# Preparing the last stage's first rows between two weight conversions, and taking two low planes to VectorE

## The chip, the cores and the metric

The kernel runs on one NeuronCore of a Trainium2 chip. The metric is the device time of one execution in microseconds (us). TensorE is PE in the profile, VectorE DVE, ScalarE ACT, GpSimd POOL, and SyncE SP; SP computes nothing here and requests most of the DMAs.

## The reference

A causal attention (4 batches, 12 heads, 448 positions, head dimension 64) gives 1792 rows of 768 numbers. A mixture of experts sends each row to one of 8 experts, and a last dense layer follows. Cut to what matters:

```python
x = softmax(q k^T / 8, causal) v                 # 1792 x 768
for e in range(8):                               # rows of expert e
    out[mask] = gate_w * eom * (relu(x[mask] @ w1[e]) @ w2[e])
h = out @ w_in                                   # 768 x 2048, float64 weights
y = (h - tanh(h)) @ w_out                        # 2048 x 768, float64 weights
```

## The kernel before

Each float32 operand is held as two float16 planes, a high one and a low one (the remainder), and each product is three float16 products. Work on PE goes in tiles of 128 rows.

The kernel has three stages in time: attention, experts, dense layer. In the expert stage the rows of an expert are handled in slots of 128 rows. `slot` (L815 and after) computes one slot: 144 matmuls with the expert's first weights (`slot_mm1`, tiles `ph`), the rectifier on ACT (L169, tile `hh`) with its remainder on DVE (L170, tile `hl`), and 48 matmuls with the second weights (`slot_mm2`, tiles `py`), whose result ACT copies (L831) and SP stores into `ys_d`, a buffer in device memory (L858). Slots past an expert's first ones stand in nested conditionals (`extra`, L871); expert 7 runs two slots here, one static and one `extra`.

The dense layer's weights come as 24 units of 128 x 1024 float64 numbers. A unit is loaded (`conv_load`, L906), turned into float32 by bit operations on DVE (`to_f32`, L896, L899, L902, through the buffer `cc`), scaled into its high plane (L113 on ACT or L117 on DVE), and its low plane is formed by `rest_of`: one DVE instruction (L121), or two on POOL for each half (L115 into the scratch `scm`, then the subtraction L129). `conv_store` (L917) writes 22 of the units back to `wb_d` in device memory. `conv` is all of this for one unit. The last two units are loaded on POOL's DMA queue into `stg` (named `wo` in the trace), and stay on the chip.

The order around the change is the order in which the program writes the instructions; each engine runs its own in that order. In front of expert 7 stands a conditional loop for leftover units (`remaining`, L1077); its body does not run with these inputs, but each engine takes the jump around it. The three 128-row blocks that the dense layer begins with (group 0) are requested by `prep0` (L971). During expert 7's static slot, `fill(1)` converts one unit, `fill(2)` requests the last two units and converts the second, and `fill(3)` runs `first_prep`: per block a maximum (L982), five short instructions for a scale (L984 to L989), the high plane on ACT (L996), the low plane in two halves on POOL (L1010, L1012), and short scale work on DVE (L1016 to L1025). Behind the slot SP requests the first chunk of the dense layer's first weights (`wi_load`, L955, two planes into `raw`) from `wb_d`, and the rows of group 1.

After the `extra` slot the block at L1181 to L1189 converts the last two units on DVE. Then PE transposes group 0 (L149, copied by ACT L153 and DVE L151), and the dense layer starts: `a_mm(n)` (L1222) makes the 16 tiles of a group, and DVE, ACT and POOL compute the cubic-like activation of each tile (DVE L1230 first, POOL L1232 and L1235, DVE L1242, L1248, L1250). The second product (L1273) of a group runs beside the first product of the next.

Of the kernel before, what the change touches and what calls it, by code (L numbers as in the profile page):

```python
# [12 lines left out]
F32 = mybir.dt.float32  # L13
# [3 lines left out]
U32 = mybir.dt.uint32  # L17
AF = mybir.ActivationFunctionType
ALU = mybir.AluOpType
AX = mybir.AxisListType  # L20
PSUM = bass.MemoryType.PSUM
SP = mybir.EngineType.SP
# [7 lines left out]
NBLK = NT // 128  # L30
# [16 lines left out]
NDY = 22  # L47
# [10 lines left out]
def build(ctx: ExitStack, tc: tile.TileContext, kq0, kq, v, wg, wo, w1, w2, wf, out):  # L58
# [26 lines left out]
    cst0 = cst.tile([1, E], I32, name="cst0")  # L85
    xtab = cst.tile([1, UOFF[-1]], I32, name="xtab")
    flg = cst.tile([1, 4], I32, name="flg")

    xTs = {"n0": cst.tile([128, 2, KD, 128], F16, name="xT_n0")}

# [817 lines left out]
    def conv(src, hi, lo, eng="v"):  # L908
        hs = [slice(0, 512), slice(512, 1024)]
        to_f32([(cc[:, h], src[:, h, :]) for h in hs])  # L910
        for h in hs:
            scaled("a", hi[:, h], cc[:, h].bitcast(F32))
        for h in hs:
            rest_of(eng, lo[:, h], cc[:, h].bitcast(F32), hi[:, h])
# [149 lines left out]
    def order_b():  # L1064
        px = mp_t.tile([128, 512], F32, tag="t", name="order")[:, 0 : 5 * NBLK]
        for c in range(NC_):
            nc.tensor.matmul(out=px, lhsT=oba[:, c, :], rhs=obb[:, c].rearrange("p n z -> p (n z)"), start=(c == 0),
                             stop=(c == NC_ - 1))
        pv = px.rearrange("p (n z) -> p n z", z=5)
        nc.vector.tensor_reduce(out=smt[:, :, 0:1], in_=pv[:, :, 0:2], op=ALU.add, axis=AX.X)  # L1070
        nc.vector.tensor_reduce(out=smt[:, :, 1:2], in_=pv[:, :, 2:5], op=ALU.add, axis=AX.X)

    wts = {0: wts0, 1: wts1 + w_tiles(1, (1,))}
    tl = tail()

    def remaining():
        with tc.If(tot < NDY):  # L1077
            with tc.For_i(tot, NDY, 1) as o:
                conv_load(stg[0], o)
                conv(stg[0], stg[2][:, 0:1024], stg[2][:, 1024:2048])  # L1080
                nc.sync.dma_start(out=wb_d[:, :, ds(o, 1), :].rearrange("p a o n -> p a (o n)"),
                                  in_=stg[2][:, 0:2048].rearrange("p (a n) -> p a n", a=2))

    cntrs = []
    for e in range(E):
        if e == 0:
            slot_rows(0, 2, 1)
            slot_rows(1, 0, "n")
        slot_rows(e, 2 + FB[e], 0)
        if e == 0:  # L1090
            for _ in range(4):
                next(tl, None)
        if e + 1 < E:
            if e:
                wts[e + 1] = w_tiles(e + 1)

            def fill_hi(z, e=e):
                todo = PLANS[e]
                if e:
                    pieces_hi(wts[e + 1], sum(todo, [])[CUT[z] : CUT[z + 1]])  # L1100
                else:
                    pieces_hi(wts[e + 1], todo[max(z - 1, 0)] if z != 1 else [])

            def fill_lo(z, e=e):
                if e == 0 and z >= 2:
                    next(tl, None)
                pieces(wts[e + 1], PLANS[e][z], e + 2, False)
                if e == 1 and z in (1, 3):
                    order_a(2) if z == 1 else order_b()

            fill = (fill_hi, fill_lo)
        else:
            wo_ = [w16s[0][z].tile([128, KF2, DM], F16, tag=tg, name=f"wo_{z}") for z, tg in enumerate(("w1", "w2"))]
            wof = [t.rearrange("p k f -> p (k f)") for t in wo_]
            stg = [wof[0][:, z * 4096 : (z + 1) * 4096].bitcast(U32).rearrange("p (n t) -> p n t", t=2) for z in range(2)]
            stg += [wof[1][:, z * 2048 : (z + 1) * 2048] for z in range(2)]
            tot = nc.values_load(flg[0:1, 1:2], min_val=0, max_val=NDY)
            remaining()
            first["yg"] = [wof[1][:, z * 2 * DM : (z + 1) * 2 * DM].bitcast(F32) for z in range(3)]
            at_ = (wof[1][:, 6 * DM :], wof[0])  # L1120
            first["yq"] = [[t[:, z * 2 * DM : (z + 1) * 2 * DM].rearrange("p (k x n) -> p k x n", k=KD, x=2)
                            for z in range(3)] for t in at_]
            first["dg"] = [[t[:, 6 * DM + 256 * z : 6 * DM + 256 * (z + 1)].bitcast(BF16).rearrange(
                "p (a n) -> p a n", a=2) for z in range(3)] for t in at_]
            first["sc"] = [t[:, 6 * DM + 768 : 6 * DM + 832].bitcast(F32) for t in at_]
            second = nc.values_load(flg[0:1, 0:1], engines=(SP,), min_val=0, max_val=128)
            for i in range(GB[0]):
                prep0(0, i, second * i if i else 0)

            def fill(z):  # L1130
                if z == 2:
                    for q in range(2):
                        conv_load(stg[q], NDY + q, nc.gpsimd)
                if z in (1, 2):
                    conv(cu[z - 1], co[z - 1][:, 0], co[z - 1][:, 1], "p")
                    conv_store(z - 1, nc.values_load(flg[0:1, z + 1 : z + 2], engines=(SP,), min_val=0, max_val=NDY - 1))
                if z == 3:
                    first_prep()

        if e == 0:  # L1140
            cntrs += [nc.values_load(cnt[0:1, x : x + 1], min_val=0, max_val=NT) for x in range(E)]
        cntr = cntrs[e]
        hint(e, 1 + FB[e])
        slot(e, FB[e], wts[e], f"n{e % 2}", fill,
             ((1, (FB[e] + 1) % 2),) + ((("n", f"n{(e + 1) % 2}"),) if e + 1 < E else ()),
             [lambda j=j: slot_rows(*j) for j in ((e + 1, 1, 1), (e + 2, 0, "n")) if j[0] < E], late=e + 1 == E)
        if e == 0:
            for _ in tl:
                pass
            sctx.close()  # L1150
            cv = w16ctx.enter_context(tc.tile_pool(reuse_waits="tile", name="cv", bufs=1, side="right"))
            cu = [cv.tile([128, 1024, 2], U32, name=f"cu_{z}") for z in range(2)]
            cc = cv.tile([128, 1024], U32, name="cc")
            co = [cv.tile([128, 2, 1024], F16, name=f"co_{z}") for z in range(2)]
            cuf = [t.rearrange("p n t -> p (n t)").bitcast(F16) for t in cu]
            cof = [t.rearrange("p a n -> p (a n)") for t in co]
            ccf = cc.bitcast(F32)
            ny = KD * 384
            spare = [t[:, ny:4096].bitcast(F32) for t in cuf]
            yg1 = cof[1][:, 0 : 2 * DM].bitcast(F32)  # L1160
            dgs = [cof[1][:, 1536 + 256 * z : 1792 + 256 * z].bitcast(BF16).rearrange("p (a n) -> p a n", a=2) for z in range(2)]
            rss = [cof[0][:, 768 * z : 768 * (z + 1)].bitcast(BF16).rearrange("p (a n) -> p a n", a=2) for z in range(2)]
            sc = [cof[0][:, 1536 + 64 * z : 1600 + 64 * z].bitcast(F32) for z in range(2)]
            G = {0: {"yh": cuf[0][:, 0:ny].rearrange("p (k n) -> p k n", k=KD),
                     "yl": cuf[1][:, 0:ny].rearrange("p (k n) -> p k n", k=KD), "rs": rss[0]}}
            oba = cof[1][:CP, 0 : NC_ * 128].bitcast(BF16).rearrange("p (c n) -> p c n", n=128)
            ob = ccf[:CP, 0 : 3 * NC_ * NBLK].bitcast(BF16)
            obm = ob[:, 0 : NC_ * NBLK].rearrange("p (c n) -> p c n", c=NC_)
            obb = ob[:, NC_ * NBLK :].rearrange("p (c n z) -> p c n z", c=NC_, z=5)
            order_a(0)  # L1170
            order_a(1)
            conv_load(cu[0], 0)
            conv_load(cu[1], unit_of(1, 1))
        if e == E - 1:
            wi_load(nc.sync, 0)
            for i in range(GB[1]):
                prep0(1, i, second * (GB[0] + i))
        extra(e, 1 + FB[e], wts[e])
    qc = (cc, wof[0][:, 8192:10240].bitcast(U32))
    qhl = [[y[:, (10 + q) * 1024 : (11 + q) * 1024] for y in wof] for q in range(2)]  # L1180
    for q in range(2):  # L1181
        to_f32([(qc[q], stg[q])])
        scaled("v", qhl[q][0], qc[q].bitcast(F32))
        if q:
            for prep in (prep2, prep3):
                for i in range(GB[0]):
                    tpool[0] = (mp_t, mp_y, mp_h)[i]
                    prep(0, i, "tys"[i])
        rest_of("p", qhl[q][1], qc[q].bitcast(F32), qhl[q][0])  # L1189

    mctx.close()
    gt = [w16s[1][z].tile([128, 2, KF2, 384], F16, tag=tg, name=f"g_{z}") for z, tg in enumerate(("w1", "w2"))]
# [10 lines left out]
    fp_o = wctx.enter_context(tc.tile_pool(reuse_waits="tile", name="fp_o", bufs=2, space=PSUM))  # L1203
    tpool[0] = wctx.enter_context(tc.tile_pool(reuse_waits="tile", name="fp_t", bufs=2, space=PSUM))

    oidx = yp.tile([128, NBLK, 2], U32, name="oidx")
    for z in range(2):
        nc.gpsimd.tensor_scalar(out=oidx[:, :, z], in0=smt[:, :, 0], scalar1=2.0, scalar2=float(z), op0=ALU.mult, op1=ALU.add)
    Q = {}
    ro = fp_o.tile([128, 512], F32, tag="o", name="ro")  # L1210
    for i in range(GB[0]):
# [171 lines left out]
```

## Time and profile before

| | |
|---|---|
| median of 3 runs | 1044.98 us (1041.18 to 1048.73) |
| profiled execution | 1040.45 us, span 1038.7 us |
| PE busy | 984.5 us, 95% of the span |
| DVE busy | 786.6 us, 76% |
| ACT busy | 596.7 us, 57% |
| POOL busy | 472.2 us, 45% |
| mean granted clock of TensorE | 0.993 |

The profile shows one execution. A row of the timeline gives the start from the beginning of the span, the length, the engine, the line, what is written and read, and in square brackets how long the engine had been idle and what released it. Rows of windows give what each engine was busy for in a stretch, then the granted clock of TensorE, then the share of the DMA engines' time and their rate.

### The profile page before, as it was taken

The numbers are of one execution on the slowest core, as the hardware profiler recorded it, in microseconds if no ns is written. First come the engines' busy times: TensorE is split into PE (matmuls) and PEld (weight loads), VectorE is DVE, ScalarE is ACT, GpSimd is POOL, SyncE is SP. The second block draws the span as 40 slices with busy tenths as digits, with TensorE's granted clock in tenths as the row PEclk, the third lists the DMA queues.
The fourth block names the chain that finished last, engine by engine and source line by source line (L and its number), as shares of the span: only waits on it lengthen the run. The fifth ranks groups of instructions, "written<-read, shape, count | busy, mean of one in ns | idle before, by whom it ended". The sixth has DMA issues, their size and how long they took to land. (4 is left out here: it accounts for less than half of the span.)

```text
span 1038.7 us, 24100 instructions
## 1 busy us (share of the span) xinstructions
PE 984.5 (95%) x9177; PEld 743.4 (72%) x9177; DVE 786.6 (76%) x1609; ACT 596.7 (57%) x1194; POOL 472.2 (45%) x499
## 2 busy tenths in 40 slices
PE   5999999998998999999988889999999999999996
PEld 4999999996876878777865555666666666667763
DVE  6668778786786778778877899887888798776640
ACT  5777776764456366564332679555656566555530
POOL 5475876585311011102137789545544443443321
PEclk9999999999999999999999999999999999999999
DMA  8989997963888979977987514010011000000000
GB/s 240 234 216 270 241 266 202 240 197 126 303 342 316 351 268 333 363 291 239 317 299 280 209 62 157 24 47 16 24 31 32 9 31 9 16 16 17 16 24 23
DMA packets 62646, 173.92 MB, mean 167 GB/s; under 512 B 8368, under 2 KB 23344, under 8 KB 59424
## 3 DMA queue, kind: packets, MB, share of 16 engines
q1 hardware_dynamic: 56352, 147.20, 42.7%
q0 software_dynamic: 6144, 24.84, 8.3%
q8 instruction: 79, 1.29, 0.5%
q14 instruction: 71, 0.58, 0.2%
HBM read 132.30 MB, written 29.62 MB: 156 GB/s over the span
## 5 line engine op out<-in xcount | busy, mean ns | idle before, releaser
L1273 PE MATMUL fo<-wo,g 128*128 128x384 f16 x1344 | 228.2, 326 | 0.0
L1222 PEld LDWEIGHTS <-raw 128*128 128x128 f16 x1440 | 140.7, 98 | 87.9 <-issue 9.5
L1273 PEld LDWEIGHTS <-g 128*128 128x128 f16 x1344 | 131.2, 98 | 83.8
L1232 POOL TENSOR_TENSOR V<-cu,cc 128x384 f32<-128x384 f32 (+1 forms) x80 | 78.7, 984 | 189.0 <-ACT cu L1231 188.2
L162 PEld LDWEIGHTS <-w 128*128 128x128 f16 x2592 | 148.9, 99 | 15.5 <-issue 14.4
L1222 PE MATMUL fh<-cu,raw 128*128 128x384 f16 (+1 forms) x864 | 131.9, 308 | 5.7 <-DVE cc L1230 5.7
L344 ACT ACTIVATE P<-s,nb 112x112 f32<-112x112 f32 (+1 forms) x192 | 89.9, 495 | 56.5 <-DVE nb L338 27.9
L381 PE MATMUL o<-v,PT 112*112 112x65 f32 x960 | 114.6, 259 | 0.0
L381 PEld LDWEIGHTS o<-v,PT 112*112 112x112 f32 x960 | 105.4, 178 | 0.1
L121 DVE SCALAR_TENSOR_TENSOR w<-raw,w 128x768 f16<-128x768 f32 (+1 forms) x99 | 99.1, 1061 | 3.6 <-ACT w L113 3.6
L799 POOL DMA_INDIRECT xg<-xs_d,idx x22 | 27.5, 1249 | 162.2 <-PEq L871 21.6
L1231 ACT ACTIVATE cu<-cc 128x384 f32<-128x384 f32 (+1 forms) x80 | 40.1, 502 | 101.9 <-DVE cc L1230 101.9
L1235 POOL TENSOR_TENSOR X<-cc,X 128x384 f32<-128x384 f32 (+1 forms) x80 | 91.2, 1141 | 4.1 <-ACT X L1234 0.5
L1230 DVE TENSOR_TENSOR cc<-fh,co 128x384 f32<-128x384 f32 (+1 forms) x80 | 42.0, 526 | 66.3 <-PE fh L1222 50.7
L113 ACT ACTIVATE w<-raw 128x768 f16<-128x768 f32 (+2 forms) x106 | 89.0, 904 | 5.5 <-DVE xi L758 3.2
L331 DVE TENSOR_REDUCE s<-s 112x2 f32<-112x224 f32 (+1 forms) x144 | 78.9, 548 | 14.8 <-PE s L327 12.7
L1242 DVE SCALAR_TENSOR_TENSOR V<-cu,V 128x384 f32<-128x384 f32 (+1 forms) x80 | 85.3, 1066 | 0.1
L1250 DVE TENSOR_TENSOR V<-V,co 128x384 f32<-128x384 f32 (+1 forms) x64 | 78.4, 1224 | 0.0
L1222 PE MATMUL fh<-yh,raw 128*128 128x384 f16 x384 | 67.6, 326 | 0.7 <-DVE cc L1230 0.7
L1251 ACT ACTIVATE g<-V 128x384 f16<-128x384 f32 (+1 forms) x80 | 40.1, 501 | 46.9 <-DVE V L1250 46.7
L362 PE MATMUL t<-ident,P 112*112 112x112 f32 x480 | 66.7, 262 | 0.0
L325 PE MATMUL s<-kh,qa 128*112 128x112 f16 (+1 forms) x192 | 54.7, 293 | 12.7 <-POOL qa L276 7.4
(657 smaller groups left out, 2038.8 us busy)
## 6 DMA issues: line engine op xcount, KB each, us to landing
raw<-w SPq DMA_DIRECT2D x48, 512.0 KB
raw<-w SPq DMA_DIRECT2D x60, 384.0 KB
cu<-wf SPq DMA_DIRECT2D x22, 1024.0 KB
wb_d<-co SPq DMA_DIRECT2D x22, 512.0 KB
raw<-kq SPq DMA_DIRECT2D x11, 896.0 KB
raw<-wb_d SPq DMA_DIRECT2D x8, 768.0 KB
xs_d<-xq SPq DMA_DIRECT2D x24, 224.0 KB
raw<-v SPq DMA_DIRECT2D x11, 448.0 KB
```

Source lines behind the costliest of these rows:

```text
L113: nc.scalar.activation(out=out, in_=in_, func=AF.Copy, scale=WS)
L121: nc.vector.scalar_tensor_tensor(out=out, in0=in_, scalar=WS, in1=hi, op0=ALU.mult, op1=ALU.subtract)
L162: nc.tensor.matmul(out=ph[:, (f % 4) * 128 : (f % 4 + 1) * 128], lhsT=w[0][:, ww, k, f * 128 : (f + 1) * 128], rhs=xTs[tag][:, xx, k, :], ...
L331: nc.vector.tensor_reduce(out=d["nm", m], in_=d["s", m], op=ALU.max, axis=AX.X, negate=True)
L344: nc.scalar.activation(out=d["P"][:, j, OFF[i] : OFF[i] + n], in_=d["s", m][:, z, :], func=AF.Exp, bias=d["nb"][:, 2 * i + j : 2 * i + j + ...
L381: nc.tensor.matmul(out=po[:, i, :], lhsT=d["PT"][:, g, o : o + CP], rhs=d["t"][3][:, hl, j, :], start=(j == 0), stop=(j == i))
L1222: nc.tensor.matmul(out=ph[:, 0:nt], lhsT=wi[ww][:, f // 4, k, f % 4 * 128 : (f % 4 + 1) * 128], rhs=yy[:, k, 0:nt], start=(q == 0), stop=( ...
L1232: nc.gpsimd.tensor_tensor(out=d["V"], in0=d["U"], in1=d["h"], op=ALU.mult)
L1235: nc.gpsimd.tensor_tensor(out=d["X"], in0=d["h"], in1=d["X"], op=ALU.subtract)
L1242: nc.vector.scalar_tensor_tensor(out=d["V"], in0=d[f"S{z}"], scalar=QD[z - 1], in1=d["V"], op0=ALU.add, op1=ALU.mult)
L1250: nc.vector.tensor_tensor(out=d["V"], in0=d["V"], in1=rs_y(g, nt), op=ALU.mult)
L1273: nc.tensor.matmul(out=po[:, 0:384], lhsT=t[:, x, k, i * 128 : (i + 1) * 128], rhs=wo_[ww][:, k, z * 384 : (z + 1) * 384], start=(k == 0 a ...
```

## The change

The three requests of group 0's rows come ahead of the conditional for leftover units; so that their buffer is not written by the loop, the loop's output goes to `spo`, another part of the weight buffer. `first_prep` moves from `fill(3)` to `fill(2)`, and the second conversion from `fill(2)` to `fill(3)`. The low planes of the last two units go from POOL to DVE, behind the transposes of group 0. The index table `oidx` for the output's scatter is made during expert 1.

```diff
+    oidx = cst.tile([128, NBLK, 2], U32, name="oidx")
...
+        for z in range(2):                       # now in order_b
+            nc.gpsimd.tensor_scalar(out=oidx[:, :, z], in0=smt[:, :, 0], scalar1=2.0, scalar2=float(z), op0=ALU.mult,
+                                    op1=ALU.add)
...
-                conv(stg[0], stg[2][:, 0:1024], stg[2][:, 1024:2048])
+                conv(stg[0], spo[:, 0:1024], spo[:, 1024:2048])
...
-            stg += [wof[1][:, z * 2048 : (z + 1) * 2048] for z in range(2)]
-            tot = nc.values_load(flg[0:1, 1:2], min_val=0, max_val=NDY)
-            remaining()
+            spo = wof[0][:, 8192:10240]
...
             for i in range(GB[0]):
                 prep0(0, i, second * i if i else 0)
+            tot = nc.values_load(flg[0:1, 1:2], min_val=0, max_val=NDY)
+            remaining()
 
             def fill(z):
                 if z == 2:
                     for q in range(2):
                         conv_load(stg[q], NDY + q, nc.gpsimd)
-                if z in (1, 2):
-                    conv(cu[z - 1], co[z - 1][:, 0], co[z - 1][:, 1], "p")
-                    conv_store(z - 1, nc.values_load(flg[0:1, z + 1 : z + 2], engines=(SP,), min_val=0, max_val=NDY - 1))
-                if z == 3:
                     first_prep()
+                if z in (1, 3):
+                    b = z // 2
+                    conv(cu[b], co[b][:, 0], co[b][:, 1], "p")
+                    conv_store(b, nc.values_load(flg[0:1, b + 2 : b + 3], engines=(SP,), min_val=0, max_val=NDY - 1))
...
         scaled("v", qhl[q][0], qc[q].bitcast(F32))
-        if q:
-            for prep in (prep2, prep3):
-                for i in range(GB[0]):
-                    tpool[0] = (mp_t, mp_y, mp_h)[i]
-                    prep(0, i, "tys"[i])
-        rest_of("p", qhl[q][1], qc[q].bitcast(F32), qhl[q][0])
+    for prep in (prep2, prep3):
+        for i in range(GB[0]):
+            tpool[0] = (mp_t, mp_y, mp_h)[i]
+            prep(0, i, "tys"[i])
+    for q in range(2):
+        rest_of("v", qhl[q][1], qc[q].bitcast(F32), qhl[q][0])
```

POOL's instructions in expert 7's static slot, before: the requests of the last two units (`wo<-wf`), the second unit's low plane (`co_4959`), then the blocks' low planes (`wo_17684`), of which the first half is shown.

```order
L906 DMA wo_17683<-wf 128x2048 x2
L115 TENSOR_SCALAR scm<-cc 128x512
L129 TENSOR_TENSOR co_4959<-scm,co_4959 128x512
L115 TENSOR_SCALAR scm<-cc 128x512
L129 TENSOR_TENSOR co_4959<-scm,co_4959 128x512
L1010 TENSOR_SCALAR scm<-wo_17684 128x384
L1012 TENSOR_TENSOR wo_17684<-scm,wo_17684 128x3x128
```

And POOL in the changed kernel, the end of the same place (the second unit is `co_4960` here, the blocks `wo_17687`):

```order
L1011 TENSOR_SCALAR scm<-wo_17687 128x384
L1013 TENSOR_TENSOR wo_17687<-scm,wo_17687 128x3x128
L116 TENSOR_SCALAR scm<-cc 128x512
L130 TENSOR_TENSOR co_4960<-scm,co_4960 128x512
L116 TENSOR_SCALAR scm<-cc 128x512
L130 TENSOR_TENSOR co_4960<-scm,co_4960 128x512
```

The second unit's low plane has moved behind all six halves of the blocks' low planes.

SP's instructions at the conditional, before: the end of the loop's body and the jump (L1078, L1077), then the three requests of rows.

```order
L1078 COMPARE_AND_BRANCH
L1078 UNCONDITIONAL_BRANCH
L1077 UNCONDITIONAL_BRANCH
L1126 TENSOR_LOAD flg
L1126 ISA x2
L971 DMA wo_17684<-ys_d 128x768
L971 ISA
L971 DMA wo_17684<-ys_d 128x768
L971 ISA
L971 DMA wo_17684<-ys_d 128x768
```

And SP in the changed kernel, up to the conditional's comparison (L1081):

```order
L1128 TENSOR_LOAD flg
L1128 ISA x2
L972 DMA wo_17687<-ys_d 128x768
L972 ISA
L972 DMA wo_17687<-ys_d 128x768
L972 ISA
L972 DMA wo_17687<-ys_d 128x768
L1131 TENSOR_LOAD flg
L1131 ISA x2
L1081 COMPARE_AND_BRANCH
```

The three requests have moved from behind the jump to a place ahead of its comparison; what follows on SP (two stores of units, the slot's store, `wi_load`, the rows of group 1) stands in the same order as before.

## Rows read from the trace of the kernel before

**Rows 1.** The page, the whole execution.

```profile
span 1038.7 us, 24100 instructions
```

**Rows 2.** Waits of PE: who waited for whom, us in total, times, longest.

```profile
PE py_I-18271_18272 L174 <- ACT hh_I-18095_18096 L169: 4.1, 1, 4.1
```

**Rows 3.** Timeline of PE: end of the extra slot, start of `a_mm`.

```profile
560.64 0.82 PE L174 MATMUL py_I-18271_18272<-w,hh_I-18095_18096 128*128 128x384 f16 x2 [4.07 <-ACT hh_I-18095_18096 L169]
...
574.50 8.94 PE L1222 MATMUL fh<-cu,raw 128*128 128x384 f16 x54
```

**Rows 4.** Windows: behind the wait, and late in group 0.

```profile
560.60:564.00 3.40, 3.35 (x11) 1.39 (x12) 2.89 (x5) 1.18 (x2) 3.10 (x4) 0.50 0.73 274
...
595.50:633.00 37.50, 33.95 (x220) 20.13 (x220) 37.50 (x59) 31.82 (x65) 33.18 (x31) 1.00 0.26 97
```

**Rows 5.** Timeline of ACT: high planes of group 0.

```profile
557.52 2.59 ACT L996 ACTIVATE wo<-wo 128x768 f16<-128x768 f32 x3 [5.63 <-issue]
```

**Rows 6.** Timeline of DVE: block preparation, last units, first tiles of group 0.

```profile
555.48 0.95 DVE L982 TENSOR_REDUCE wo<-wo 128x1 f32<-128x768 f32 x1 [2.96 <-DMA wo<-ys_d]
...
557.28 0.16 DVE L989 TENSOR_TENSOR wo<-wo,smt 128x3 f32<-128x3 f32 x1
...
565.08 1.82 DVE L902 SCALAR_TENSOR_TENSOR cc<-wo,cc 128x1024 uint32<-128x1024 uint32 x1
...
577.72 0.56 DVE L1230 TENSOR_TENSOR cc<-fh,co 128x384 f32<-128x384 f32 x1 [3.00 <-POOL scm L115]
...
581.30 0.92 DVE L987 TENSOR_SCALAR wo<-wo 128x3 f32<-128x3 f32 x1
...
582.47 0.70 DVE L989 TENSOR_TENSOR wo<-wo,smt 128x3 f32<-128x3 f32 x1
...
585.66 1.35 DVE L1242 SCALAR_TENSOR_TENSOR V<-S,V 128x384 f32<-128x384 f32 x1 [0.42 <-POOL V L1232]
```

**Rows 7.** Timeline of POOL: requests, low planes of the blocks and units.

```profile
548.38 1.18 POOL L906 DMA_DIRECT2D wo<-wf  x2
...
557.61 0.59 POOL L1010 TENSOR_SCALAR scm<-wo 128x384 f32<-128x384 f32 x1 [3.15 <-issue]
...
561.30 0.59 POOL L1010 TENSOR_SCALAR scm<-wo 128x384 f32<-128x384 f32 x1
561.97 0.91 POOL L1012 TENSOR_TENSOR wo<-scm,wo 128x384 f16<-128x384 f32 x1
562.98 1.00 POOL L1010 TENSOR_SCALAR scm<-wo 128x384 f32<-128x384 f32 x1
564.06 1.76 POOL L1012 TENSOR_TENSOR wo<-scm,wo 128x384 f16<-128x384 f32 x1
...
569.75 1.76 POOL L1012 TENSOR_TENSOR wo<-scm,wo 128x384 f16<-128x384 f32 x1
...
573.88 1.16 POOL L129 TENSOR_TENSOR wo<-scm,wo 128x512 f16<-128x512 f32 x1
575.13 0.62 POOL L115 TENSOR_SCALAR scm<-cc 128x512 f32<-128x512 f32 x1
```

**Rows 8.** Timeline of SP's queue: stores and loads as they are requested.

```profile
546.61 1.56 SPq L971 DMA_DIRECT2D wo<-ys_d  x3
...
559.95 0.56 SPq L917 DMA_DIRECT2D wb_d<-co  x1
...
563.43 0.83 SPq L955 DMA_DIRECT2D raw<-wb_d  x2
```

**Rows 9.** Line L1077 (the conditional) on SP: instruction, count, ns, first and last start.

```profile
L1077 SPq EVENT_SEMAPHORE  x2: 17/17/17, 545.6 to 545.7; - x2
...
L1077 SPq COMPARE_BRANCH  x1: 50/50/50, 541.6 to 541.6; - x1
```

**Rows 10.** Windows: a stretch of back-to-back loads; the last number is GB/s.

```profile
567.00:570.00 3.00, 3.00 (x21) 1.76 (x18) 2.97 (x3) 0.00 (x0) 2.73 (x4) 1.00 0.99 409
```

**Rows 11.** Groups by line: busy us, mean ns of one, idle before.

```profile
L121 DVE SCALAR_TENSOR_TENSOR w<-raw,w 128x1024 f16<-128x1024 f32 x41 | 48.1, 1216 | 0.0
```

More of the change, by code (lines that the diff above doesn't have):

```diff
@@ L1079, in remaining @@
                 conv_load(stg[0], o)
-                conv(stg[0], stg[2][:, 0:1024], stg[2][:, 1024:2048])
+                conv(stg[0], spo[:, 0:1024], spo[:, 1024:2048])
                 nc.sync.dma_start(out=wb_d[:, :, ds(o, 1), :].rearrange("p a o n -> p a (o n)"),
-                                  in_=stg[2][:, 0:2048].rearrange("p (a n) -> p a n", a=2))
+                                  in_=spo.rearrange("p (a n) -> p a n", a=2))
     cntrs = []
@@ L1204, in build @@
     tpool[0] = wctx.enter_context(tc.tile_pool(reuse_waits="tile", name="fp_t", bufs=2, space=PSUM))
-    oidx = yp.tile([128, NBLK, 2], U32, name="oidx")
-    for z in range(2):
-        nc.gpsimd.tensor_scalar(out=oidx[:, :, z], in0=smt[:, :, 0], scalar1=2.0, scalar2=float(z), op0=ALU.mult, op1=ALU.add)
     Q = {}
```

## The prediction

> **What bounds the kernel now.** I read the table of engines first: PE is busy for 95% of the span, so only a place where PE stands still, or where another engine sets the pace, can give or cost time. Then the waits of PE: one of 4.1 us stands at the place of this change [rows 2]. In PE's timeline it is the wait ahead of the extra slot's second product, 4.07 us to 560.64 [rows 3], and the window behind it shows a granted clock of 0.50 for 3.40 us, the lower of the two levels (1.2 instead of 2.4 GHz), so another 1.7 us of work lost [rows 4].
>
> Followed back: ACT's rectifier is queued behind three high planes of group 0, which begin at 557.52 [rows 5]; these wait for DVE's scale, ready at 557.44, behind a reduction that waited 2.96 us for the third block of rows [rows 6]. SP requests the rows from 546.61 on [rows 8], as it loses 4.0 us at the conditional, 541.6 to 545.6 [rows 9].
>
> What counts, though, is when DVE gets the first dense tile, at 577.72 [rows 6]: late in group 0 DVE is busy for 37.50 of 37.50 us [rows 4], so the group is DVE's from there, and a shift of that start goes 1:1 into the end. That start is a_mm(0) at 574.50 [rows 3] plus 3.22.
>
> **What the change does there.** *Rows earlier.* SP requests the blocks at about 541.7 instead of 546.61, 1.56 us for three. The third's reduction began 7.3 us after its request (555.48 - 548.17) beside POOL's loads, which are requested at 548.38 [rows 6 to 8]; a store of a unit is followed by its dependant after 3.48 (559.95 to 563.43 [rows 8]). From 543.3 the third block thus lands between 546.8 and 550.6; I take 547.1, since those loads still come behind the jump, now about 544.1 to 548.1. Adding 1.96 (555.48 to 557.44) the scale is ready at 549.0, and ACT is through with the high planes at 551.6 (2.59 [rows 5]). The second conversion now stands behind that on DVE; its three operations, 1.82 each at most [rows 6], end by about 557.3, the rectifier by about 558.5. PE's stall shrinks from 4.07 to about 2.2, and the drop of the clock there goes with it. PE is done with the slot some 3.5 us earlier.
>
> *The second unit later.* This is the price. On POOL the second unit's low plane now stands behind six halves of the blocks' low planes, and SP's store of that unit, requested at 559.95 before, waits for it. `wi_load` stands behind that store on SP and must see it land in `wb_d`. POOL is free for the halves at about 549.45 (jump, and the two loads of 1.18). A pair (scratch, subtraction) alone costs 0.59 + 0.91 + 2 x 0.08 = 1.66. Beside DVE's work on the last units three pairs took 562.98 to 571.51, 2.84 each [rows 7]. A half of the unit costs 0.62 + 1.16 + 0.16 = 1.94 alone, 3.3 at the same ratio. Bounds of POOL's end P: all alone 549.45 + 6 x 1.66 + 2 x 1.94 = 563.3; all contended 549.45 + 6 x 2.84 + 2 x 3.3 = 573.1. I go by who runs beside it: first pair alone to 551.1; three beside the second conversion on DVE, partly in turn, 2.3 each, to 558.0; two alone to 561.3; the unit's halves beside DVE's last-unit block, which now starts near 560.7, 2 x 3.3: P = 567.9.
>
> What contention does is in the rows: the same subtraction takes 0.91 at 561.97 and 1.76 at 564.06, and DVE's operation beside it 1.82 [rows 6, 7], one waiting out the other. The Trainium skill ("SBUF — State Buffer", section "SBUF: two separate sides") says that VectorE and GpSimd share a port pair by an exclusive lock held for a whole instruction, not by splitting bandwidth. By that rule POOL ends at about 567.9 here; were the load only a proportional slowing at the small share DVE needs, P would be nearer 563.3. The trace agrees with the lock, 1.76 against 0.91.
>
> From P on: store requested at 568.0, `wi_load` at 568.0 + 3.48 = 571.5. Its first plane: the 0.52 MB store needs 1.28 at 409 GB/s [rows 10], so 2.2 of the 3.48 are fixed; 2.2 + 0.786 MB / 409 GB/s (1.9) = 4.1. So a_mm(0) starts at 575.6 instead of 574.50: the 3.5 us that PE gains at the slot become a wait for weights. PE then stands idle for about 5 us ahead of a_mm(0), longer than the 4.07 that the half clock followed, so I charge the same 1.7 once more. First tile on DVE: 575.6 + 3.22 + 1.7 = 580.5, **+2.75**.
>
> *Low planes on DVE.* Four POOL operations of L115 and four of L129 leave the stretch 573.1 to 580.9. DVE's scale work of group 1 no longer waits in turn with them: 0.92 - 0.16 and 0.70 - 0.16 for two short operations, and 0.42 of waiting for V [rows 6], together **-1.7** (at worst 0). DVE gains 2 x 1.22 = 2.4 us [rows 11]; they lie while DVE has nothing (it idled 3.00 us ahead of 577.72 [rows 6]). If that cover is gone, +2.4.
>
> *`oidx`.* Two short POOL operations move from the dense layer's start to expert 1, where POOL is not waited for: 0.
>
> Sum: 2.75 - 1.7 = **+1.0**. The profiled execution took 1040.45 (span 1038.7 [rows 1]), so 1041.5 by its measure; the median of the runs, 1044.98, lies 4.53 above it: **1046.0**. With P at 563.3, `wi_load` goes out at 566.9, a_mm(0) would be at 571.0 without a drop of the clock: first tile -3.5, sum -5.2, 1039.8. With P at 573.1: a_mm(0) at 580.8, first tile +8.0, sum +6.3, 1051.3.
>
> **The rivals.** *The gain survives.* If POOL ends early enough that weights are never waited for, a_mm(0) comes 4.07 + 1.7 earlier, at 568.7; with the relief -5.8 - 1.7 = -7.5: 1037.5. It needs `wi_load` at about 564.6, so P near 561.0. For it: POOL's pairs take only 1.66 alone, and half the stretch is without DVE. Against: even uncontended I get 563.3, unless POOL starts earlier than 549.45. Chance 0.20, with the partial cases between.
>
> *Slower: preparation is no earlier, and the unit is stuck behind it.* DVE, ACT and POOL now all have group 0's preparation ahead of the second conversion. Should the rows land as late as before (scale at 557.4, because requests ahead of the jump gain nothing), POOL begins the pairs at 557.6 as it did [rows 7], and P = 557.4 + 19 = 576.4 at the contended and uncontended mix taken above (567.9 - 549.0): a_mm(0) at 584.1, PE stopped for about 10 us, +11: 1056. It decides from the time of DVE's third reduction: each us behind 547 is a us of the end. Against: SP's comparison, at 541.6, stands behind the requests now, and the 4.0 us of the jump is what delayed them [rows 9]. Chance 0.08; this is also the case that the change does not do what it says.
>
> *DVE's low planes uncovered.* If weights come early, DVE itself is late: its last-unit block plus 2.4 us with the first tile waiting: 2.4 on top of +1.0: 1048.4. For it: DVE is the pace of group 0. Against: PE is what waits, by the forecast, till 575.6. Chance 0.10.
>
> **How the numbers follow.** Forecast 0.62, gain 0.20, slower side 0.08, DVE 0.10. The range: below to the gain's 1037.5 and somewhat under it, 1036, above past the contended bound of 1051.3 and the DVE case, with the runs' spread, 1053; it leaves out the 1056 and half of the gain's tail. One per cent, 10.4 us, is about what a measurement of this kernel can tell from no change. Faster by more than that would need more than the whole stall and the relief: 0.05. Slower by more needs rows clearly late: 0.07. Within: 0.88.
>
> **What would show it.** Right: the three requests on SP at about 541.7; the third reduction at 546 to 548; a stall of about 2 us ahead of the extra slot's second product, without a half clock behind it; POOL's last subtraction of the second unit ending near 568, that unit's store right behind, `wi_load` near 571.5; PE waiting for `raw` ahead of a_mm(0) near 575.6, at half clock behind; DVE's first tile near 580.5, its scale operations of 0.2 thereafter. Wrong: POOL ending by 562 (the gain survives), the third reduction past 553 (slower), or DVE busy without a gap up to the first tile (its low planes are the bound).

## The result, and the profile after

The changed kernel took 1052.05 us (median of 13 runs) against 1045.86 for the kernel before, run beside it on the same chips. The ratio is 1.0062, with a 95% interval of 1.0035 to 1.0089: 6.5 us slower (3.7 to 9.3). The trace of the profiled execution spans this, against 1038.7 before [rows 1]:

```profile
span 1045.8 us, 24080 instructions
```

So the profiles differ by 7.1 us. One row serves as a common clock, the first product of the extra slot on PE, in the timeline of the kernel before and then of the changed one:

```profile
547.70 4.18 PE L162 MATMUL ph_I-18101_18102<-xT,w 128*128 128x128 f16 x72
```

```profile
548.74 4.18 PE L163 MATMUL ph_I-18104_18105<-xT,w 128*128 128x128 f16 x72
```

1.0 us of the 7.1 had come about before that row. Now the changed kernel's queue of SP, beside [rows 8]:

```profile
543.36 0.97 SPq L972 DMA_DIRECT2D wo<-ys_d  x2
...
548.76 0.35 SPq L972 DMA_DIRECT2D wo<-ys_d  x1
...
570.49 0.55 SPq L918 DMA_DIRECT2D wb_d<-co  x1
...
573.63 0.83 SPq L956 DMA_DIRECT2D raw<-wb_d  x2
574.72 1.61 SPq L972 DMA_DIRECT2D wo<-ys_d  x3
583.94 0.36 SPq L859 DMA_DIRECT2D ys_d<-yo_I-18102_18103  x1
```

Two blocks of rows are requested at 543.4 and 544.0, the third only at 548.8, later than before. The second unit's store goes out at 570.49 (559.95 before), the first weights' load at 573.63 (563.43), and the extra slot's own store at 583.94. The conditional itself costs SP hardly anything now, in the rows of its line (instruction, count, ns, first and last start), beside [rows 9]:

```profile
L1081 SPq EVENT_SEMAPHORE  x2: 17/17/17, 550.0 to 550.1; - x2
...
L1081 SPq COMPARE_BRANCH  x1: 50/50/50, 549.8 to 549.8; - x1
```

549.8 to 550.0, where it was 541.6 to 545.6. The 4 us have not gone, they stand ahead of the third request. POOL, beside [rows 7]: the start of the blocks' first half, the two operations of the third half, the end of the last half, and the second unit's last subtraction.

```profile
554.01 0.58 POOL L1011 TENSOR_SCALAR scm<-wo 128x384 f32<-128x384 f32 x1 [2.17 <-issue]
...
557.98 1.42 POOL L1011 TENSOR_SCALAR scm<-wo 128x384 f32<-128x384 f32 x1
559.48 1.22 POOL L1013 TENSOR_TENSOR wo<-scm,wo 128x384 f16<-128x384 f32 x1
...
565.14 0.91 POOL L1013 TENSOR_TENSOR wo<-scm,wo 128x384 f16<-128x384 f32 x1
...
568.80 1.66 POOL L130 TENSOR_TENSOR co<-scm,co 128x512 f16<-128x512 f32 x1
```

POOL is done with the unit at 570.46. DVE, beside [rows 6]:

```profile
551.87 0.95 DVE L983 TENSOR_REDUCE wo<-wo 128x1 f32<-128x768 f32 x1 [2.36 <-DMA wo<-ys_d]
...
553.67 0.16 DVE L990 TENSOR_TENSOR wo<-wo,smt 128x3 f32<-128x3 f32 x1
...
568.75 0.70 DVE L897 TENSOR_SCALAR cc<-wo 128x1024 uint32<-128x1024 uint32 x1 [4.50 <-POOL scm L116]
...
583.31 0.56 DVE L1231 TENSOR_TENSOR cc<-fh,co 128x384 f32<-128x384 f32 x1 [2.28 <-PE fh L1223]
586.59 2.67 DVE L983 TENSOR_REDUCE wo<-wo 128x1 f32<-128x768 f32 x3 [2.72 <-SPq L872]
...
590.19 0.55 DVE L1231 TENSOR_TENSOR cc<-fh,co 128x384 f32<-128x384 f32 x1
```

Two waits are new. The last units' conversion stands still for 4.50 us, because its first operation writes the buffer `cc`, out of which POOL still reads the second unit. And behind the first dense tile DVE waits 2.72 us for SP (L872 is the line of the conditional around the extra slot, and a q behind an engine's name stands for its instruction queue). SP in turn had stood ahead of the extra slot's store (L859) until the rows of group 1 had landed, in the waits of its queue (us in total, times, longest):

```profile
SPq L859 <- DMA wo<-ys_d: 7.0, 2, 3.9
```

The same reductions and the second dense tile before:

```profile
578.19 2.66 DVE L982 TENSOR_REDUCE wo<-wo 128x1 f32<-128x768 f32 x3
...
583.09 0.55 DVE L1230 TENSOR_TENSOR cc<-fh,co 128x384 f32<-128x384 f32 x1
```

The account: first tile 583.31 - 577.72 = +5.6; reductions 586.59 - 578.19 = +8.4; second tile 590.19 - 583.09 = +7.1, which is the difference of the spans. From there both kernels run alike. PE, beside [rows 2, 3]:

```profile
562.51 0.82 PE L175 MATMUL py_I-18274_18275<-w,hh_I-18098_18099 128*128 128x384 f16 x2 [4.90 <-ACT hh_I-18098_18099 L170]
...
577.89 1.14 PE L1223 MATMUL fh<-cu,raw 128*128 128x384 f16 x6 [2.05 <-DVE cu L152]
579.74 9.33 PE L1223 MATMUL fh<-cu,raw 128*128 128x384 f16 x48 [0.71 <-DMA raw<-wb_d]
```

The stall that the change was to remove is longer, 4.90 for 4.07, and a_mm(0) waits for DVE's copies (which stand behind the 4.50) and again for the second plane of the weights. The first plane was as late: a_mm(0)'s first weight load (PEld) waited for it too, 2.06 us to 577.72, where the copies ended at 577.84. In the waits of PEld (us in total, times, longest):

```profile
PEld L1223 <- DMA raw<-wb_d: 3.2, 2, 2.1
```

So two paths end together there, and both start at POOL's last pair: the copies behind its last read of `cc`, the weights behind its last subtraction. The windows behind the stall and up to the first dense tile show mean granted clocks of 0.58 and 0.68, so each has a stretch at the lower level (columns as in [rows 4]):

```profile
562.50:566.00 3.50, 3.49 (x13) 1.52 (x14) 1.75 (x3) 1.15 (x2) 3.14 (x5) 0.58 0.03 7
...
577.90:583.30 5.40, 4.69 (x20) 2.29 (x20) 3.14 (x4) 0.00 (x0) 0.00 (x0) 0.68 0.74 297
```

### The profile page after: what moved, and what is told of

Same layout as the page of the kernel before. It is cut to its first block, busy times and chain, and to the rows that moved or that the text cites. A ratio compares the mean times of both kernels' runs of the same rounds, so it can differ in the third digit from the quotient of the medians.

```text
span 1045.8 us, 24080 instructions
## 1 busy us (share of the span) xinstructions
PE 985.3 (94%) x9177; PEld 742.7 (71%) x9177; DVE 783.8 (75%) x1611; ACT 596.8 (57%) x1194; POOL 461.8 (44%) x491
```

## The experiments

"The swap" is the move of `first_prep` ahead of the second conversion. Each kernel was timed against the kernel before on the same chip; ratios are to it. e7 was run once, for its trace. The common-clock row lies anywhere between 546.2 and 556.8 from one profile to another, so verdicts rest on the ratios, and profiles on distances and waits.

| run | what | ratio | 95% interval |
|---|---|---|---|
| the change | | 1.0062 | 1.0035 to 1.0089 |
| e1_noswap | without the swap | 0.9987 | 0.9951 to 1.0023 |
| e2_swap | the swap alone | 1.0081 | 1.0045 to 1.0116 |
| e3_vlow | low planes on DVE alone | 1.0000 | 0.9965 to 1.0035 |
| e4_c1v | change, unit's low plane on DVE | 0.9999 | 0.9968 to 1.0029 |
| e5_group1_rows | change, group 1's rows earlier on SP | 1.0063 | 1.0029 to 1.0097 |
| e6_pool_order | change, POOL's order undone | 1.0049 | 1.0019 to 1.0079 |
| e8_row0_pool | change, first block on POOL's queue | 1.0055 | 1.0026 to 1.0084 |
| e10_c1v_row0 | e4 and e8 together | 1.0020 | 0.9990 to 1.0050 |
| e11_trim | change, four assertions fewer on SP | 1.0014 | 0.9984 to 1.0043 |
| e12_c1v_trim | e4 and e11 together | 0.9982 | 0.9946 to 1.0018 |

### Which part of the change costs the time

**e1_noswap**: the changed kernel, `fill` as before.

```diff
-                    first_prep()
-                if z in (1, 3):
-                    b = z // 2
+                if z in (1, 2):
...
+                if z == 3:
+                    first_prep()
```

> The change without its swap: the second conversion stays ahead of the blocks' preparation; rows early, low planes of the last units on DVE. Theory (the loss comes from POOL reaching the second unit's low plane last, so that its store, 570.5 instead of 560.0 in the trace, and everything behind that store on SP come 10 us late): the store is requested at 555 to 560 again, the first dense matmul stands at 570 to 573, no 2.7 us wait of DVE ahead of group 1's reductions; 3 to 6 us faster than before, 10 to 13 faster than the change. Rival (the 2.4 us of low planes on DVE, or the rows' requests, cost the time): 2 to 7 us slower than before, as the change.

The loss is gone. No gain can be told from noise, and the 3 to 6 us were too much: DVE still begins the last units at 562.93 and shares them with POOL, so a_mm(0) stands at 574.68, not at 570 to 573. The third request stands still here as in the change (it goes out at 550.6), so that late rows alone cost nothing that can be told from noise.

**e2_swap**: the kernel before with the edit of `fill` alone.

```diff
+                    first_prep()
-                if z in (1, 2):
+                if z in (1, 3):
```

> The kernel before with the swap alone: rows requested behind the conditional, low planes of the last units on POOL. Theory: the scale is ready at 557.4 as before, POOL works off six halves and then the second unit by about 574, the store goes out there, DVE's last units wait for the shared buffer until about 572; 8 to 14 us slower than before, worse than the change. Rival (DVE's low planes are the cost): within 2 us of before.

8.5 us slower (4.7 to 12.1): the loss of the whole change, as far as the intervals tell. The same wait for POOL stands ahead of the last units, in DVE's timeline:

```profile
573.67 0.69 DVE L896 TENSOR_SCALAR cc<-wo 128x1024 uint32<-128x1024 uint32 x1 [4.49 <-POOL scm L115]
```

**e3_vlow**: the kernel before with the low planes of the last units on DVE.

```diff
-        rest_of("p", qhl[q][1], qc[q].bitcast(F32), qhl[q][0])
+    for q in range(2):
+        rest_of("v", qhl[q][1], qc[q].bitcast(F32), qhl[q][0])
```

> The kernel before with only the low planes of the last two units on DVE, behind the transposes. Theory: they lie in DVE's 3.0 us of idleness ahead of its first dense tile, and two short operations no longer wait for POOL: 0 to 1.7 us faster than before, first dense tile at 577.7 or up to 0.5 later. Rival (the low planes delay DVE): 2.4 us or more slower.

No change; a cost of 2.4 us (1.0023) is inside the interval's reach and can't be excluded by the ratio alone. The profile speaks against it: the two operations end at 577.5, and DVE then still waits for PE.

```profile
576.25 1.22 DVE L121 SCALAR_TENSOR_TENSOR wo<-wo 128x1024 f16<-128x1024 f32 x1
578.26 0.56 DVE L1230 TENSOR_TENSOR cc<-fh,co 128x384 f32<-128x384 f32 x1 [0.79 <-PE fh L1222]
```

So the swap is what costs, and the rest of the change is neutral within its interval (-5.1 to +2.4 us, e1).

### What the swap makes late

**e4_c1v**: the changed kernel with POOL relieved of the second unit's low plane.

```diff
-                    conv(cu[b], co[b][:, 0], co[b][:, 1], "p")
+                    conv(cu[b], co[b][:, 0], co[b][:, 1], "pv"[b])
```

> The change with the second unit's low plane on DVE instead of POOL, the swap kept. Theory: the store needs POOL no more and goes out at about 563 to 565 instead of 570.5, the shared buffer is free at about 563, the first dense matmul stands at 572 to 575, DVE has no wait for SP ahead of group 1's reductions; 0 to 4 us faster than before, 6 to 11 faster than the change, though DVE does 1.3 us more. Rival (DVE's added work is the cost): slower than the change by about 1.3.

The swap is kept, DVE does more, and the loss is gone. The store goes out at 563.97, and the last units no longer wait for POOL (SP, then DVE):

```profile
563.97 0.55 SPq L918 DMA_DIRECT2D wb_d<-co  x1
```

```profile
566.03 0.91 DVE L897 TENSOR_SCALAR cc<-wo 128x1024 uint32<-128x1024 uint32 x1 [0.42 <-DVEq L872]
...
582.70 2.67 DVE L983 TENSOR_REDUCE wo<-wo 128x1 f32<-128x768 f32 x3 [1.15 <-SPq L872]
```

The place was right, in two details not: a_mm(0) stood at 577.81, though the clock row was 2.2 us later too, and 1.15 us of waiting for SP stayed. With e2 this shows the link: the swap costs while the second unit's low plane shares POOL with the blocks, and no longer once it is on DVE.

**e6_pool_order**: the changed kernel with the blocks' low planes behind the unit's on POOL; DVE and ACT keep the swap.

```diff
-        for j in range(GB[0]):
-            prep_lo(0, 0, GB[0], j, "p")
...
+                if z == 3:
+                    first_lo()
```

> The change with one thing undone on POOL alone: the six halves of the blocks' low planes stand behind the second unit's low plane, and not ahead of it; DVE and ACT keep the changed order. Theory (POOL's order makes the loss): the unit's store goes out at about 565 to 567 instead of 570.5, the shared buffer is free at 564, the first dense matmul stands at 574 to 576; 2 to 5 us faster than the change, 1 to 4 slower than before. Rival (the order on DVE and ACT, or the rows): as the change.

The unit's store went out at 558.25, yet most of the loss stayed (2.0 to 8.3 us). POOL now idles for 5.73 us until DVE has converted the unit, and works on the blocks until 572.94; PE's transposes of the blocks wait for that:

```profile
573.05 0.82 PE L150 MATMUL pt_I-19420_19421<-identh,wo 128*128 128x128 f16 x6 [7.71 <-POOLq L872]
```

POOL's order only chooses who waits for its last operation: store and buffer in the change, PE here. My theory, as far as it put the loss on the order on POOL alone, falls with this run; what costs is that POOL has both jobs late.

**e5_group1_rows**: the changed kernel; group 1's rows requested between `first_prep` and the second conversion.

```diff
+                    if b:
+                        for i in range(GB[1]):
+                            prep0(1, i, second * (GB[0] + i))
```

> The change with the three requests of group 1's rows moved on SP from behind the first weights' load to between the blocks' preparation and the second conversion. Theory: in the change these requests go out at 574.7, their landing holds back the extra slot's store to 583.9 and the end of the conditional on SP to 586.6, for which DVE waits 2.7 us; requested near 566 instead, this wait is gone and DVE takes up group 1's reductions right behind its first dense tile: 2 to 3 us faster than the change, 3 to 5 slower than before. Rival (DVE's wait is the rows' own transfer or the 2.4 us of low planes): no change against the change.

DVE's wait for SP is gone, but not the time: now the weights come later, the first product waits for them and a second time for what the profile puts under SP, and the first tile is at 586.44.

```profile
580.13 1.14 PE L1224 MATMUL fh<-cu,raw 128*128 128x384 f16 x6 [1.84 <-DMA raw<-wb_d]
582.55 15.50 PE L1224 MATMUL fh<-cu,raw 128*128 128x384 f16 x84 [1.28 <-SPq L872]
```

The 2.72 us were one of two paths from the same late store, not a cost by itself. A miss.

### Why the rows were late

**e8_row0_pool**: the changed kernel with the first block on POOL's queue.

```diff
-                prep0(0, i, second * i if i else 0)
+                prep0(0, i, second * i if i else 0, nc.sync if i else nc.gpsimd)
```

> The change with the first block requested on POOL's queue, so that SP requests two blocks and two instructions fewer stand on it ahead of the third block. In the change SP stood still from 544.5 to 548.7 ahead of the third request with its wait over, and one instruction packet moved on the DMA queues in that time. Theory (SP waits for its own instructions at a fixed place in its stream, at the jump before and ahead of the third request now): the third request now falls ahead of that place, both of SP's requests go out within 1 us, the standstill comes behind them, the third reduction starts at 547 to 549 instead of 551.9, and the second unit's store goes out 1 to 3 us earlier; 1 to 3 us faster than the change. Rival (the request waits for a landing or for a full queue): the standstill stays ahead of the last of SP's requests, no gain.

Neither as told: the standstill still stands ahead of SP's last request (545.6 to 552.1), now between its address move and the request. The rows of the request's line, of the change and of e8 (kind, count, ns, first and last start):

```profile
L972 SPq EVENT_SEMAPHORE  x3: 17/17/28, 543.3 to 544.5; - x3
...
L972 SPq MOVE wo<-ys_d x2: 29/29/29, 543.9 to 548.7; - x2
```

```profile
L972 SPq MOVE wo<-ys_d x2: 29/31/33, 545.0 to 545.6; - x2
L972 SPq DMA_DIRECT2D wo<-ys_d x2: 342/342/342, 545.0 to 552.1; - x2
```

Counted from the load of the rows' address (three instructions at L1128), eleven instructions lie ahead of the standstill in both: the edit had taken away one instruction net, and the standstill moved by that one. That left both theories standing, and no time was gained (1.0055, the change 1.0062).

**e7_tot_first**: the changed kernel; another register load (three instructions) ahead of the requests.

```diff
+            tot = nc.values_load(flg[0:1, 1:2], min_val=0, max_val=NDY)
             second = nc.values_load(flg[0:1, 0:1], engines=(SP,), min_val=0, max_val=128)
...
-            tot = nc.values_load(flg[0:1, 1:2], min_val=0, max_val=NDY)
```

> The change with one more register load (three instructions on SP) ahead of the three requests, taken from behind them. In every changed kernel so far SP stood still at the same count, behind the eleventh instruction from the load of the second rows' address. Theory (SP waits for the next piece of its own instructions, at a fixed place in the stream): the standstill of 4 to 5 us moves forward by three instructions, to right ahead of the second request, or its address move. Rival (it waits for something that the third request needs): it stays ahead of the third request.

The standstill moved ahead of the second request: its address move is at 550.7, the request itself at 554.14, and the third follows at once.

```profile
L972 SPq MOVE wo<-ys_d x2: 29/29/29, 550.7 to 554.7; - x2
```

```profile
554.14 0.96 SPq L972 DMA_DIRECT2D wo<-ys_d  x2
```

It is a place in SP's stream of instructions, not a wait of the third request. That SP waits for instructions there is an inference from the DMA queues: in 550.8 to 554.1, beside the data, one packet of a queue of instructions moved.

```profile
q14 instruction: 1, 0.01, 0.6%
```

The other traces bear the inference out. In all thirteen profiles, at the jump or ahead of a request, one packet of this queue moves in the standstill, and SP goes on 1.5 to 1.6 us after that packet's start, whether the standstill lasts 3.1 us (e2) or 6.5 (e8).

**e11_trim**: the changed kernel with four bounds assertions fewer on SP, so that the requests stand ahead of that place.

```diff
-            second = nc.values_load(flg[0:1, 0:1], engines=(SP,), min_val=0, max_val=128)
+            second = nc.values_load(flg[0:1, 0:1], engines=(SP,), min_val=0, max_val=128,
+                                    skip_runtime_bounds_check_because="0 or 128")
```

(The other three are at the load of the first row of experts 4 to 6.)

> The change with four bounds assertions left out on SP (three upstream, one at the address of the second rows), nothing else. Theory (fixed place): all three requests fall ahead of the standstill and go out within 1.5 us; the third reduction starts 3 us earlier against the extra slot's matmuls than in the change, POOL still begins with the loads of the last units behind the jump, so its end and the second unit's store gain only about 2 us: 1 to 3 us faster than the change, still 3 to 5 slower than before. Rival (late rows are the whole loss, as the slower case of the prediction had it): as fast as before or faster.

All three requests go out within 2.57 us, and the standstill is back at the conditional, 4.0 us, as in the kernel before:

```profile
547.13 2.57 SPq L973 DMA_DIRECT2D wo<-ys_d  x3
```

```profile
L1082 SPq EVENT_SEMAPHORE  x2: 17/17/17, 554.4 to 554.5; - x2
...
L1082 SPq COMPARE_BRANCH  x1: 50/50/50, 550.4 to 550.4; - x1
```

PE's stall ahead of the extra slot's second product falls to 1.10 us and DVE's wait for SP to 0.98:

```profile
565.01 0.50 PE L175 MATMUL py_I-18246_18247<-w,hh_I-18070_18071 128*128 128x384 f16 x2 [1.10 <-ACT hh_I-18070_18071 L170]
```

```profile
587.80 2.67 DVE L984 TENSOR_REDUCE wo<-wo 128x1 f32<-128x768 f32 x3 [0.98 <-SPq L873]
```

With the swap untouched the kernel is 1.5 us slower than before (-1.7 to +4.5), so the edit gives back some 5 of the 6.5 us, more than I expected; the two intervals together leave about 1 to 9. This profile's slot also begins late (555.03), which flatters its waits; the ratio has no such help. Two things stay open. The waits behind POOL are still there, 4.42 us for DVE's last units and 3.05 ahead of a_mm(0), so the chain is shortened and not gone. And the edit shifts all of SP's instructions behind it, so that the 5 us are shown for the edit; that all of them are the third block's is argued.

**e10_c1v_row0** and **e12_c1v_trim** join e4's edit with that of e8 and of e11.

> The change with both repairs: the second unit's low plane on DVE, and the first block requested on POOL's queue. Theory: scale ready near 551, the rectifier of the extra slot near 558, so that PE hardly waits and keeps its clock; store of the second unit near 559; first dense matmul at 571 to 573; 3 to 5 us faster than before, 9 to 12 faster than the change. Rival (DVE's own work ahead of the first dense tile is the bound, whatever comes early): same as before within 1.5 us, as with the first repair alone.

> The same four assertions left out, with the second unit's low plane on DVE. Theory: rows early and POOL relieved, the rectifier of the extra slot waits for nothing but PE, so PE's wait ahead of its second product falls below 1.5 us and its clock stays; first dense matmul 3 to 4 us earlier against the extra slot's start than with the low plane on DVE alone; 2 to 5 us faster than before. Rival (DVE's own work bounds the first dense tile): same as before within 1.5 us.

e10 has late rows, as e8, and comes out as e4 does within the intervals. e12 has both links cut: PE waits 1.62 us, just above what I gave it, and the first dense product stands at 572.59. Against the slot's start (549.67) it comes 22.9 us behind, where it came 26.8 behind before. It is the fastest median measured, 1039.93, but its interval holds 1: it beats the change, not demonstrably the kernel before. Nor can it be told from e4 (0.9982 and 0.9999): once POOL is relieved, early rows bring nothing that shows.

```profile
560.16 0.50 PE L175 MATMUL py_I-18244_18245<-w,hh_I-18068_18069 128*128 128x384 f16 x2 [1.62 <-ACT hh_I-18068_18069 L170]
...
572.59 5.68 PE L1225 MATMUL fh<-cu,raw 128*128 128x384 f16 x34
```

## Why the prediction was right, and where its sizes were off

- **Path: right.** The second unit's low plane behind the blocks on POOL, its store late, the weights behind the store, PE's gain turned into a wait: the trace has each of these. That POOL's load makes the loss is shown by e2 and e4, by making it without the rest of the change and by taking it away alone; that the late store is its only way is not so, as e6 has the store early and most of the loss.
- **Rows at 547.1: the step that failed.** The price was taken from [rows 9] as one of the conditional. It is one of a place in SP's instructions, and the change put the third request behind it: 548.76, block reduced at 551.87, scale ready at 553.83 instead of 549.0. The rival that named this (each us behind 547 is a us of the end) had its mechanism right and its cause wrong; by its rule the 4.8 us at the third reduction turn the +1.0 into +5.8. Its own 1056 leaves out the relief of 1.7 that the other sums have. With the requests ahead of that place, e11 measures +1.5 us (-1.7 to +4.5), where the sum was +1.0.
- **POOL's end 567.9: 570.46.** It began 4.6 us late (554.01, not 549.45) and made up 2.0, since DVE's last units, which were to contend with it, waited for it instead: the unit's two halves took 4.3, where 6.6 were charged. Where both run, the halves show 1.42 and 1.22 for 0.59 and 0.91, again one operation waiting out the other. The lock that the Trainium skill describes ("SBUF — State Buffer", section "SBUF: two separate sides") agrees with these rows.
- **Stall 2.2: 4.90.** The rows were late, and ACT's two planes of the second unit now stand ahead of the rectifier as well. The drop of the clock was to go with the stall; it stayed (a mean of 0.58 over 3.50 us behind the stall, 0.50 over 3.40 before).
- **a_mm(0) at 575.6: 577.89,** 7.4 us behind the end of POOL's unit (7.7 in the sum). But two paths of that length lead there, 0.12 us apart at their ends; the one over the shared buffer `cc` and DVE (4.50) was not in the prediction.
- **First tile +2.75: +5.6.** From a_mm(0) it took 5.4 us, against 3.22 + 1.7 = 4.9 in the sum; the clock was 0.68, so some 1.7 of 5.4 was lost to it as charged, and the second plane's 0.71 is the rest, in part within the 1.7.
- **Not in the prediction: DVE's 2.72 us for SP.** The rows of group 1, requested behind the weights, hold back the extra slot's store to 583.94; DVE goes on at 586.59, when SP has passed the end of the conditional.
- **Relief -1.7: -1.3.** From the reductions to the second tile 3.60 us, before 4.90. The 0.42 of waiting for V did not go.
- **Low planes of 2.4 us covered: held.** DVE waits for PE behind them by 2.28 us here and by 0.79 in e3. `oidx` was not tried alone; e1 contains it.

So +1.0 was forecast and +6.5 measured; e11's edit, which takes the requests ahead of the standstill, gives back about 5 of it. The time lies in the stated range, but close to its upper end (1052.05 of 1053), and that the bound for full contention (+6.3) comes so near is luck: POOL ended at 570.46, and not at that bound's 573.1, and began 4.6 us late. Of the signs named for being right, the third reduction (546 to 548, was 551.87), the stall of about 2 us and the clock behind it did not come; the late store, the late weights and the lower clock at the first dense tile did.

## What to carry to other kernels

A chain through an engine that is "not the bottleneck" is priced at its last link: before reordering that engine's work, write down who waits for its last operation, through a buffer as well as through a store. A stall at a jump may belong to the stream of instructions and not to the jump: check whether moving work past it only moves the stall. When several waits end together, taking one away shows nothing (e5); breaking the chain at an early link gave back the loss (e1, e4) or most of it (e11).

## What the runs showed of the hardware

SP stood still for 3.4 to 6.5 us at one place of its straight-line code, without an open semaphore to wait for, in each of the eight profiles that had instructions of the changed stretch there; the place followed the count of instructions (moved by three in e7, by one in e8). In the other five the standstill lay at the jump, 4.0 us in the kernel before and in e11. In all thirteen one packet of the instruction queue q14 moved, and SP went on 1.5 to 1.6 us after its start. Why the packet came as late as it did is not shown. The Trainium skill ("Runtime: NRT & Kernel Launch", section "Instruction fetch mechanics") has the sequencer fetch its next block by DMA during the current one, and counts a taken branch to a target outside its window as what breaks this. The jump's 4.0 us fit that, though no run here shows where the window ends; the standstill in straight-line code, with DMA queues busy, is one that the sequential fetch did not hide.
